# Block sums of the mixing weights by DRAM copies and adding transfers, four marking matmuls less, and a weighted product that waits

## The chip, the cores and the metric

The kernel runs on one core of a Trainium2 chip. The metric is the device time of one execution in microseconds (us), the median of several runs. TensorE (PE in the profile) does the matrix products, VectorE (DVE), ScalarE (ACT) and GpSimd (POOL) the rest; SyncE (SP) issues most transfers, ScalarE and GpSimd issue some. The engines run side by side, each its own instructions in a fixed order.

## The reference

Two branches read the normalised rows of x (2048 tokens of 512 values): a dilated local attention, and a gated MLP whose gate mixes tokens with the 2048 x 2048 weights `w_sp`.

```python
xn = _layernorm(x, axis=-1)
s = _A_ref(xn, A_wqkv, A_wo)            # 32 heads, 8 taps at a distance of 2, softmax, output product
g = _silu(_B_ref(xn, B_w_in, B_w_sp, B_b_sp, B_w_out))
return x + s * g

def _B_ref(x, w_in, w_sp, b_sp, w_out):
    z = _gelu(jnp.einsum("bsd,df->bsf", x, w_in))
    z1 = z[..., :Fh]
    z2 = _layernorm(z[..., Fh:], axis=-1)
    g = jnp.einsum("ts,bsf->btf", w_sp, z2) + b_sp[None, :, None]
    return jnp.einsum("bsf,fd->bsd", z1 * g, w_out)
```

## The kernel before

All products are made of three passes over values split in a high and a low half (`split`, L194: ScalarE makes the high half, VectorE subtracts it for the low one).

The opening (`opening`, L295, and the code around `column_tile`, L277) normalises x in 16 token tiles and turns them so that features lie on partitions. Tiles 0 to 5 are turned by TensorE. Tiles 6 to 15 come from a second, already turned copy of x (xT, L262); their means and scales are found on the rows (`row_stats`, L253), raised to a power on GpSimd (`rows_ready`, L267), stored to DRAM (`rows_out`, L240, tensor mv_d) and loaded back to all partitions (`rows_in`, L271, tile mr), in three sets: tiles 6 to 8, 9 to 12 and 13 to 15. `column_tile` then subtracts and multiplies (L280) and `low_x` (L234) makes the low half. `pair` (L427) makes the q, k and v products, group by group (g = 0, 1, 2, each with 512 columns of `wqkv`), and stores them to `qkv_d` from ScalarE's queue. TensorE takes the products in this order: group 0 for tiles 0 to 4, group 0 of tile 5 with group 1 of tiles 0 to 5, group 0 of tiles 6 to 15, group 1 of tiles 6 to 15, group 2 of all.

Then come the z1 products (L700 to L706), the z2 products (`z2_half`, L725, each half of a token tile's 896 columns in a bank: 512 and 384 wide), and the mixing with `w_sp`. The attention (`attention`, L530) runs on VectorE and GpSimd beside all of that, as a chain of operations in a fixed order (`line`); `weighted` (L618) multiplies the taps of v and notes each product in `sums_of`.

The mixing uses a scheme with seven products of blocks instead of eight: it needs, beside plain blocks of `w_sp`, four sums of blocks for each of two halves a of the output columns and each of eight token blocks. With t0, t1 for the upper and l0, l1 for the lower blocks, `added` (L390) makes

```python
for out_, p_, q_ in ((l1, t1, l1), (t1, t0, t1), (t0, t0, l1), (l0, t0, l0)):
    eng.tensor_tensor(out_, p_, q_, op=ALU.add)
```

`block_sums` (L395) loads the blocks, has them added and stores the results to `sums_d`. It is called three ways: `pool_sums` on GpSimd for six blocks of a = 1, behind column tile 12; `first_sums` on VectorE for a = 0, between the z1 products; `raw_sums` (L405) for the last two of a = 1, between the z2 products. The mixing loads the sums much later (`summed`, L872, from about 367 us on).

The mixing begins with `second_seeds` (L981): four matmuls without use of their results mark the banks of the second half (L984), and ScalarE then writes the biases into them as start values (`seed`, L843).

What sets the order: a scheduler places instructions by priority and by a simulated time line of its own, unless they are pinned (`pin`, `keep_in_program_order`) or held by a manual dependency. A transfer that nothing pins and that waits for nothing can be placed far ahead of where the code issues it. On each queue a transfer waits until the eighth before it has landed, and a queue's later transfers wait behind it.

Of the kernel before, what the change touches and what calls it, by code (L numbers as in the profile page):

```python
# [17 lines left out]
P = 128  # L18
# [39 lines left out]
def kernel(  # L58
# [330 lines left out]

    def added(ts, eng):  # L390
        t0, t1, l0, l1 = ts
        for out_, p_, q_ in ((l1, t1, l1), (t1, t0, t1), (t0, t0, l1), (l0, t0, l0)):
            eng.tensor_tensor(out_, p_, q_, op=ALU.add)  # L393

    def block_sums(a, i, tile_=None, eng=nc.vector, loads=nc.sync, stores=nc.scalar, behind=None):  # L395
        top, low = [(tile_ or t4)(f"s{n}_{a}_{i}") for n in "ab"]
        for t, r in ((top, 0), (low, HT)):
            ins = loads.dma_start(t, w_sp[2 * a : 2 * a + 2, r + i].rearrange("c p t -> p c t"))
            if behind:
                tc.add_manual_dep(ins.ins, behind[0].ins.name, behind[1], reason="sums later")  # L400
        added([top[:, 0], top[:, 1], low[:, 0], low[:, 1]], eng)
        for r, t in enumerate((top, low)):
            stores.dma_start(sums_d[a, r, i], t)

    def raw_sums(a, i):  # L405
        ts = [
            fetch(w_sp[2 * a + c, r + i], CT, f"sr_{a}_{i}_{c}_{r}") for r in (0, HT) for c in range(2)
        ]
        added(ts, nc.vector)
        for n, t in enumerate(ts):  # L410
            nc.sync.dma_start(sums_d[a, n // 2, i, :, n % 2], t)

    def early_tile(name):
        return t2(name).rearrange("p (i t) -> p i t", i=2)

    def pool_sums(a, i, tile_, *behind):
        block_sums(a, i, tile_, nc.gpsimd, nc.gpsimd, nc.gpsimd, behind)

    z1_sums = [(0, i) for i in range(HT)]

# [57 lines left out]
    for j in range(11, NT):  # L478
        if j + 2 < NT:
            fetch_cols(j + 2)  # L480
        if j == NT - 3:
            rb = raws.tile([P, 512], F32, tag="raw", name="rb", bufs=RAW)
            rbv = rb.rearrange("p (j q) -> p j q", j=JC)
            pin(nc.sync.dma_start(rbv, mv_d[:JC, 1].unsqueeze(0).to_broadcast([P, JC, P])))
        turned = column_tile(j)
        if j == 12:
            for i in range(HT - 2):
                pool_sums(1, i, early_tile, turned, SYNC)
        low_x(j - 1, cols[j - 1])
        if j % 2:  # L490
            pair(0, j - 5)
# [197 lines left out]

    def first_sums(a, i):  # L690
        block_sums(a, i, stores=nc.gpsimd)

    first_sums(*z1_sums[0])

    for f in range(FB):
        pair_ = side_pair("w1_last") if f == FB - 1 else None
        wh, wl = prep(w_in1[:, f, :], KB * P, f"w1_{f}", pair_=pair_)
        for c in range(NC):
# [11 lines left out]
            if c % 2:  # L710
                nc.scalar.dma_start(z1_d[f, c - 1 : c + 1].rearrange("c p t -> p c t"), zp)
        if f == 2:
            first_sums(*z1_sums[FB])
        if f < FB - 1:
            first_sums(*z1_sums[f + 1])

    HALF = (slice(0, 512), slice(512, FH))
    WID = (512, FH - 512)
    w2 = {
        (k, h): prep(w_in2[:, k, HALF[h]], WID[h], f"w2_{k}_{h}")  # L720
        for h in range(2)
# [3 lines left out]
    def z2_half(j, h, zt):  # L725
        xh, xl = xn_at(j)
        pz = mm(f"z2_{j}_{h}")[:, : WID[h]]
# [10 lines left out]
    def z2_stats(i, zts):  # L738
# [5 lines left out]
        mean, rstd = [mvz[:, i : i + HT + 1 : HT, n] for n in range(2)]  # L744
        nc.vector.tensor_scalar(rstd, rstd, EPS, None, op0=ALU.add)
        nc.gpsimd.tensor_tensor(rstd, rstd, nhalf.to_broadcast([P, 2]), op=ALU.pow)
# [33 lines left out]
    for i in range(HT + 2):  # L780
        if i in (1, 3):
            raw_sums(1, HT - 2 + i // 2)
        if i < HT:
# [76 lines left out]
    def plain(a, c, r):  # L860
        def w(s):
            js = r * HT + s
            pair_ = spatial.get((2 * a + c, js)) or spatial_block(2 * a + c, js)
            if (a, c, js) == (0, 0, 6):
                tc.add_manual_dep(
                    sums_of[9].ins, lows[-1].ins.name, NOSYNC, reason="first weights ahead"
                )
            return pair_

        return w  # L870

    def summed(a, half_, i):  # L872
        return lambda s: prep(sums_d[a, half_, s, :, i], CT, f"ws_{a}{half_}{i}_{s}")

# [106 lines left out]
    def second_seeds():  # L981
        for f in range(ODD + 1):

            nc.tensor.matmul(  # L984
                banks[1, f], z2_block(0, f)[0], half(0), start=True, stop=True
            )
        for f in range(ODD + 1):
# [191 lines left out]
```

## Time and profile before

| | us |
|---|---|
| median of 3 runs | 697.74 |
| lowest and highest | 696.59, 699.07 |
| profiled execution | 696.54 |
| its span, first to last instruction | 694.8 |
| granted TensorE clock | 1.00 |
| HBM read, written | 122.42 MB, 59.32 MB |
| DMA packets | 182.36 MB, mean 262 GB/s |

The page gives busy time by engine, the span in 40 slices of 17.4 us, the transfers by queue (q1 is SP's, q10 ScalarE's, q0 GpSimd's), the chain of work that ended last, and the costliest groups of instructions. A row of a group reads: line, engine, operation, output and input, count, busy us and mean ns of one, then the idle time of the engine before it and what ended it. A matmul of 512 columns is shown with 0.39 us, but they overlap: in the timeline one starts every 0.227 us.

### The profile page before, as it was taken

The page shows a single profiled execution, that of the slowest core. Times are in us where ns is not written, and L with a number is a line of the kernel's source. Part 1 is how long each engine was busy: PE and PEld are TensorE (multiplying, and loading weights), DVE is VectorE, ACT ScalarE, POOL GpSimd, SP SyncE. Part 2 cuts the span into 40 slices and gives each one's busy share as a digit, 9 for nine tenths or more (in the row PEclk, how much of TensorE's full clock was granted, in tenths as well). Part 3 has the DMA queues.
Part 4 walks back from the last instruction along what each step waited for, and adds up shares of the span by engine and source line. Part 5 has one row for each costly group of instructions (what it writes and reads, how often), then busy time and mean ns, then how long its engine had stood idle before and what let it go on. Part 6 is the DMA issues. An engine that isn't in the chain of part 4 may idle for free.

```text
span 694.8 us, 9233 instructions
## 1 busy us (share of the span) xinstructions
PE 686.6 (99%) x3084; PEld 573.0 (82%) x3084; DVE 619.4 (89%) x866; ACT 277.7 (40%) x458; POOL 215.2 (31%) x242
## 2 busy tenths in 40 slices
PE   8999999999999999998999999999999999999998
PEld 7888888888888899986888888888888888888886
DVE  6776868999989989889999998999989999989775
ACT  4342234224424256865534544442334444211531
POOL 3104837372343322124123222223111201642320
PEclk9999999999999999999999999999999999999999
DMA  8769899969999865267899768667576692655796
GB/s 270 252 193 289 288 348 384 346 204 358 407 412 340 329 231 190 80 201 231 258 403 314 284 211 298 208 232 248 183 261 206 215 342 89 221 173 190 246 330 235
DMA packets 102223, 182.36 MB, mean 262 GB/s; under 512 B 9184, under 2 KB 45280, under 8 KB 102176
## 3 DMA queue, kind: packets, MB, share of 16 engines
q1 hardware_dynamic: 56624, 102.21, 43.6%
q0 software_dynamic: 13824, 52.24, 20.9%
q10 hardware_dynamic: 31728, 27.33, 11.7%
q8 instruction: 24, 0.39, 0.2%
q14 instruction: 23, 0.19, 0.1%
HBM read 122.42 MB, written 59.32 MB: 262 GB/s over the span
## 4 chain that ended last, share of the span: by engine, by line
PE 67%; DVE 13%; DMA 12%; ACT 3%; issue 3%; POOL 1%; SPq 1%; DVEq 0%; POOLq 0%; ACTq 0%
PE g L825 35%; PE b L1067 4%; PE b L1069 4%; PE b L1068 4%; PE qkv L387 4%; PE qkv L386 4%; PE qkv L385 4%; DMA sb<-in_w_sp 3%; PE s L1069 2%; PE s L1068 2%; PE s L1067 2%; DMA sums_d<-sb 2%; DVE zst L742 2%; DMA z_d<-z1t 1%; DVE xT L280 1%
## 5 line engine op out<-in xcount | busy, mean ns | idle before, releaser
L633 POOL TENSOR_TENSOR pv<-pv 128x1024 f32<-128x1024 f32 x29 | 69.6, 2399 | 96.2 <-DVE pv L620 85.9
L573 DVE TENSOR_TENSOR pr<-k,q 128x2048 f32<-128x2048 f32 x32 | 73.6, 2299 | 2.0 <-DMA k<-qkv_d 1.9
L620 DVE TENSOR_TENSOR pv<-v,lg 128x2048 f32<-128x2048 f32 x32 | 74.6, 2331 | 0.7
L580 DVE TENSOR_REDUCE lg<-pr 128x128 f32<-128x2048 f32 x32 | 73.0, 2281 | 0.1
L647 POOL DMA_DIRECT2D o_d<-tt x32 | 18.0, 562 | 138.9 <-DVE tt L646 103.8
L433 ACT ACTIVATE stage<-qkv 128x512 f32<-128x512 f32 x40 | 23.0, 590 | 30.8 <-DMA qkv_d<-stage 17.0
L807 POOL DMA_DIRECT2D ol<-o_d x32 | 17.7, 555 | 37.7 <-DVE BIG L197 11.1
L1078 ACT ACTIVATE bt<-b 128x512 f32<-128x512 f32 x16 | 9.4, 599 | 43.5 <-PE b L1069 39.4
L709 ACT ACTIVATE z1t<-z 128x512 f32<-128x512 f32 x28 | 15.5, 597 | 26.1 <-DMA z_d<-z1t 15.3
L280 DVE TENSOR_TENSOR xT<-xT,mr 128x512 f32<-128x512 f32 x20 | 14.9, 743 | 11.9 <-DMA mr<-mv_d 6.4
L732 PE MATMUL z<-w_0h,BIG 128*128 128x512 f32 x64 | 25.0, 391 | 0.0
L731 PE MATMUL z<-w_0l,BIG 128*128 128x512 f32 x64 | 25.0, 391 | 0.0
L730 PE MATMUL z<-w_0h,BIG 128*128 128x512 f32 x64 | 24.9, 390 | 0.0
L742 DVE BATCH_NORM_STATS2 zst<-zt 128x6 f32<-128x448 f32 x32 | 19.3, 613 | 6.1 <-ACT zt L733 6.0
L754 ACT ACTIVATE zt<-zt,nmz,mvz 128x896 f32<-128x896 f32 x16 | 17.5, 1129 | 18.0 <-POOL nmz L748 18.0
L638 DVE TENSOR_TENSOR pv<-pv 128x512 f32<-128x512 f32 x32 | 22.9, 716 | 0.0
L733 ACT ACTIVATE zt<-z 128x512 f32<-128x512 f32 (+1 forms) x32 | 15.9, 536 | 15.2 <-DMA sums_d<-sa 14.0
L732 PE MATMUL z<-w_1h,BIG 128*128 128x384 f32 x64 | 21.5, 336 | 0.0
L730 PE MATMUL z<-w_1h,BIG 128*128 128x384 f32 x64 | 21.5, 335 | 0.0
L731 PE MATMUL z<-w_1l,BIG 128*128 128x384 f32 x64 | 21.4, 335 | 0.0
L393 POOL TENSOR_TENSOR sb<-sa,sb 128x512 f32<-128x512 f32 x12 | 19.7, 1644 | 5.4 <-DMA sb<-in_w_sp 5.1
L195 ACT ACTIVATE BIG<-zl 128x512 fp32r<-128x512 f32 x20 | 12.5, 630 | 21.6 <-DVE zl L895 19.8
(478 smaller groups left out, 2296.2 us busy)
## 6 DMA issues: line engine op xcount, KB each, us to landing
qkv_d<-stage ACTq DMA_DIRECT2D x24, 512.0 KB
v<-qkv_d POOLq DMA_DIRECT2D x14, 704.0 KB, 5.4
k<-qkv_d POOLq DMA_DIRECT2D x13, 704.0 KB, 6.8
sums_d<-sa POOLq DMA_DIRECT2D x14, 512.0 KB, 7.8
sums_d<-sb POOLq DMA_DIRECT2D x14, 512.0 KB, 8.0
z_d<-z1t ACTq DMA_DIRECT2D x14, 512.0 KB
zl<-z_d SPq DMA_DIRECT2D x12, 512.0 KB
tr<-t_d SPq DMA_DIRECT2D x12, 384.0 KB
```

The lines of the kernel that those rows point to most:

```text
L573: line(nc.vector.tensor_tensor(pr, taps(ks[u], j0), qb.unsqueeze(1).to_broadcast([P, W, NJ * CS]), op=ALU.mult))
L580: line(nc.vector.tensor_reduce(lgs[u][:, j0 * HS : (j0 + NJ) * HS].rearrange("p i w -> p w i"), pr.rearrange("p w (i d) -> p w i d", d=DH) ...
L620: line(nc.vector.tensor_tensor(pv.rearrange("p w (i d) -> p w i d", d=DH), taps(vs[u], j0).rearrange("p w (i d) -> p w i d", d=DH), lgs[u] ...
L633: eng.tensor_tensor(pv[:, 0:4], pv[:, 0:4], pv[:, 4:8], op=ALU.add)
L730: nc.tensor.matmul(pz, xh[:, k], wh, start=k == 0, stop=False)
L731: nc.tensor.matmul(pz, xh[:, k], wl, start=False, stop=False)
L732: nc.tensor.matmul(pz, xl[:, k], wh, start=False, stop=k == KB - 1)
L742: nc.vector.bn_stats(st[:, h], zt[:, h * FQ : (h + 1) * FQ])
L825: nc.tensor.matmul(pg, z[a], w[b], start=start and i == 0, stop=stop and i == 2, skip_group_check=seeded)
L1067: nc.tensor.matmul(pp[:, cols], hi, wh, start=k == 0, stop=False)
L1068: nc.tensor.matmul(pp[:, cols], hi, wl, start=False, stop=False)
L1069: nc.tensor.matmul(pp[:, cols], lo, wh, start=False, stop=k == n - 1)
```

## The change

1. `added`, `block_sums`, `raw_sums`, `pool_sums` and `first_sums` go, with their calls. The sums get 32 DRAM tensors of 512 KB, for a, the sum n, and pairs q of token blocks. A generator lists 64 transfers: `copied` copies a block pair from `w_sp` to a sum's tensor (DRAM to DRAM, on SP), `plus` adds a block pair, or another sum, to it (an adding transfer, on GpSimd). `go_on(n)` issues the next n of them.
2. `go_on` is called behind product pairs of groups 1 and 2 (13 times), behind the z1 products (28 times) and in the z2 loop (10 times with 2). These are 61; the last three of the list, which would add sum 0 to sum 2 for a = 1 and the pairs 1 to 3, are not issued, so these three tensors hold the lower block alone.
3. The marking matmuls go. In their place the first matmul of the narrow z2 halves of tiles 6, 7, 14 and 15 covers the whole bank: the weights of k = 0 are the last 512 columns instead of the last 384, and the half lies at the bank's end.
4. A manual dependency on VectorE puts the sixteenth weighted product of the attention behind the statistics of the last pair of z2 tiles. The old one, of the tenth, goes.

```diff
-    sums_d = dram.tile([2, 2, HT, P, 2, CT], F32, name="sums_d")
+    sums_d = {
+        (a, n, q): dram.tile([2, P, CT], F32, name=f"sums_{a}_{n}_{q}")
+        for a in range(2)
+        for n in range(4)
+        for q in range(HT // 2)
+    }
...
+    def rows_of_2k(blocks_):
+        return blocks_.rearrange("s p t -> (s p t)").rearrange("(r x) -> r x", x=4 * CT)
+
+    def raw_blocks(a, n, q):
+        r, c = divmod(n, 2)
+        j = r * HT + 2 * q
+        return w_sp[2 * a + c, j : j + 2]
+
+    def copied(to, a, q, src):
+        nc.sync.dma_start(rows_of_2k(sums_d[a, to, q]), rows_of_2k(src(a, q)))
+
+    def plus(to, a, q, src):
+        nc.gpsimd.dma_start(rows_of_2k(sums_d[a, to, q]), rows_of_2k(src(a, q)), accum_op=ALU.add, max_dma_last_dim=2048)
+
+    def weight_sums():
+        t0, t1, l0, l1 = [lambda a, q, n=n: raw_blocks(a, n, q) for n in range(4)]
+        s0, s3 = [lambda a, q, n=n: sums_d[a, n, q] for n in (0, 3)]
+        rounds = (
+            ((copied, 3, l1),),
+            ((copied, 0, t0), (plus, 3, t1)),
+            ((copied, 1, t0), (plus, 0, s3)),
+            ((copied, 2, l0), (plus, 1, t1)),
+            ((plus, 2, s0),),
+        )
+        for ops in rounds:
+            for a in range(2):
+                for q in range(HT // 2):
+                    for fn, to, src in ops:
+                        yield fn, to, a, q, src
...
+    def go_on(n):
+        for fn, *args in itertools.islice(coming_sums, n):
+            fn(*args)
...
-        turned = column_tile(j)
-        if j == 12:
-            for i in range(HT - 2):
-                pool_sums(1, i, early_tile, turned, SYNC)
+        column_tile(j)
...
             pair(g, j)
             pins[0] = False
+            go_on(1)
...
+        pz = bank[:, CT - WID[h] :]
         for k in range(KB):
-            wh, wl = [w[:, : WID[h]] for w in w2[k, h]]
-            nc.tensor.matmul(pz, xh[:, k], wh, start=k == 0, stop=False)
+            wh, wl = [w[:, CT - WID[h] :] if k == 0 else w[:, : WID[h]] for w in w2[k, h]]
+            if k == 0 and j % HT >= HT - 2:
+                nc.tensor.matmul(bank, xh[:, k], w2[k, h][0], start=True, stop=False)
+            else:
+                nc.tensor.matmul(pz, xh[:, k], wh, start=k == 0, stop=False)
...
-        nc.vector.tensor_scalar(rstd, rstd, EPS, None, op0=ALU.add)
+        known = nc.vector.tensor_scalar(rstd, rstd, EPS, None, op0=ALU.add)
+        if i == HT - 1:
+            tc.add_manual_dep(sums_of[15].ins, known.ins.name, NOSYNC, reason="gate rows ahead")
...
     def second_seeds():
-        for f in range(ODD + 1):
-
-            nc.tensor.matmul(
-                banks[1, f], z2_block(0, f)[0], half(0), start=True, stop=True
-            )
         for f in range(ODD + 1):
             seed(1, f, biases[1][0])
```

Where the scheduler puts the new transfers is not where the code calls `go_on`. On SP, at the start of the program (x are the row tiles, numbered by buffer; wqkv the weights of the second group; zpad zeros for a border), before:

```order
L202 DMA x_207<-in_x 128x512
L516 DMA qkv_d<-zpad 16x8x64 x2
L202 DMA x_209<-in_x 128x512
L202 DMA x_211<-in_x 128x512
L251 DMA x_213<-in_x 128x512
L251 DMA x_215<-in_x 128x512
L251 DMA x_217<-in_x 128x512
L251 DMA x_219<-in_x 128x512
L169 DMA wqkv_0r<-in_wqkv 128x512
```

and now, at the same place on SP (sums_3_0_93 is sum 3 of pair 0, with the buffer's number):

```order
L207 DMA x_238<-in_x 128x512
L404 DMA sums_3_0_93<-in_w_sp 16x8192
L404 DMA sums_3_1_94<-in_w_sp 16x8192
L404 DMA sums_3_2_95<-in_w_sp 16x8192
L207 DMA x_240<-in_x 128x512
L404 DMA sums_3_3_96<-in_w_sp 16x8192
L404 DMA sums_3_0_109<-in_w_sp 16x8192
L404 DMA sums_3_1_110<-in_w_sp 16x8192
L207 DMA x_242<-in_x 128x512
L256 DMA x_244<-in_x 128x512
L256 DMA x_246<-in_x 128x512
L256 DMA x_248<-in_x 128x512
```

Six copies now stand between the first row tiles and the weights of the second group, which follow four rows below this piece.

Further on SP, where the first set of row statistics is stored (mv_d) and loaded back (mr), before:

```order
L262 DMA xT_327<-in_x_t 128x512
L262 DMA xT_329<-in_x_t 128x512
L262 DMA xT_331<-in_x_t 128x512
L240 DMA mv_d<-mvt_335 6x32 x4
L271 DMA mr_361<-mv_d 128x768
L251 DMA x_363<-in_x 128x512
```

and now on SP, from the last of the copies ahead of that store on:

```order
L404 DMA sums_1_3_104<-in_w_sp 16x8192
L245 DMA mv_d<-mvt_366 6x32 x4
L404 DMA sums_2_0_89<-in_w_sp 16x8192
L404 DMA sums_2_1_90<-in_w_sp 16x8192
L404 DMA sums_2_2_91<-in_w_sp 16x8192
L404 DMA sums_2_3_92<-in_w_sp 16x8192
L404 DMA sums_2_0_105<-in_w_sp 16x8192
L404 DMA sums_2_1_106<-in_w_sp 16x8192
L404 DMA sums_2_2_107<-in_w_sp 16x8192
L404 DMA sums_2_3_108<-in_w_sp 16x8192
L276 DMA mr_392<-mv_d 128x768
```

All 32 copies now stand ahead of the first load of row statistics: 24 ahead of the store and eight between the two.

On GpSimd, the powers of the three sets (mvx, 128x3, 128x4 and 128x3) stood behind each other, with the sums' loads (sa, sb) after them:

```order
L214 TENSOR_TENSOR mvx<-mvx,nhalf 128x1 x5
L267 TENSOR_TENSOR mvx<-mvx,nhalf 128x3
L267 TENSOR_TENSOR mvx<-mvx,nhalf 128x4
L267 TENSOR_TENSOR mvx<-mvx,nhalf 128x3
L398 DMA sa_0_591<-in_w_sp 128x2x512
L398 DMA sb_0_592<-in_w_sp 128x2x512
```

and now on GpSimd the third power has the last adding transfers ahead of it:

```order
L407 DMA sums_2_0_89<-sums_0_0_81 256x512
L407 DMA sums_2_1_90<-sums_0_1_82 256x512
L407 DMA sums_2_2_91<-sums_0_2_83 256x512
L407 DMA sums_2_3_92<-sums_0_3_84 256x512
L407 DMA sums_2_0_105<-sums_0_0_97 256x512
L272 TENSOR_TENSOR mvx<-mvx,nhalf 128x3
L641 TENSOR_TENSOR pv_0_1252<-pv_0_1252 128x1024
```

Six of the 29 adding transfers stand ahead of the first power, six more ahead of the second, and the other seventeen ahead of the third; each waits on GpSimd for the copy into the same tensor, and for the sum that it reads, if it reads one.

More of the change, by code (lines that the diff above doesn't have):

```diff
@@ L388, in product @@
         return pq
[L390 to L403, printed above, removed]
@@ L719 @@
     w2 = {
[L720 removed]
+        (k, h): prep(
+            w_in2[:, k, slice(FH - CT, FH) if (k, h) == (0, 1) else HALF[h]],
+            CT if (k, h) == (0, 1) else WID[h],
+            f"w2_{k}_{h}",
+        )
         for h in range(2)
@@ L862, in w @@
             js = r * HT + s
[L863 to L866, printed above, removed]
-                )
-            return pair_
+            return spatial.get((2 * a + c, js)) or spatial_block(2 * a + c, js)
         return w
     def summed(a, half_, i):
-        return lambda s: prep(sums_d[a, half_, s, :, i], CT, f"ws_{a}{half_}{i}_{s}")
+        return lambda s: prep(sums_d[a, 2 * half_ + i, s // 2][s % 2], CT, f"ws_{a}{half_}{i}_{s}")
     def operand(i, s0):
```

27 lines of the change are left out of this document (4 added, 23 removed).

## The prediction

> **What bounds the kernel now.** I read the page first: the busy shares, the 40 slices, and the shares of the chain.
>
> ```profile
> PE 686.6 (99%) x3084; PEld 573.0 (82%) x3084; DVE 619.4 (89%) x866; ACT 277.7 (40%) x458; POOL 215.2 (31%) x242
> ...
> DMA  8769899969999865267899768667576692655796
> GB/s 270 252 193 289 288 348 384 346 204 358 407 412 340 329 231 190 80 201 231 258 403 314 284 211 298 208 232 248 183 261 206 215 342 89 221 173 190 246 330 235
> ...
> PE 67%; DVE 13%; DMA 12%; ACT 3%; issue 3%; POOL 1%; SPq 1%; DVEq 0%; POOLq 0%; ACTq 0%
> ```
>
> TensorE is busy nearly all the time, and two thirds of the chain are its own matmuls. The other third has to be looked for where TensorE waits. All its waits, from the view of who waited for whom:
>
> ```profile
> PE g L825 <- ACT g L843: 1.9, 1, 1.9
> PE warm L290 <- POOL ident masks.py:199: 1.3, 1, 1.3
> PE xt L228 <- DVE mvx L213: 0.7, 1, 0.7
> PE qkv L308 <- ACT BIG L229: 0.2, 1, 0.2
> PE g L825 <- ACT BIG L195: 0.2, 1, 0.2
> PE qkv L387 <- DVE BIG L234: 0.2, 1, 0.2
> ```
>
> After the first microseconds it waits 2.3 us in all. So a faster VectorE or emptier DMA queues can bring little, and anything that makes TensorE wait is paid in full, since its program order is fixed. Where it is nearest to waiting is the opening. The chain there, in order of time (start, us, what), is a relay of transfers and VectorE work that meets TensorE at 67.41 us:
>
> ```profile
> 24.81 0.88 POOL mvx L267
> ...
> 27.00 2.12 DMA mv_d<-mvt
> 29.13 4.68 DMA mr<-mv_d
> 33.90 0.70 DVE xT L280
> ...
> 36.74 0.60 DVE BIG L234
> ...
> 42.43 3.80 DMA mr<-mv_d
> ...
> 67.41 0.50 PE qkv L387
> ```
>
> Three times in the opening the row statistics go through a power on GpSimd (L267), a store to DRAM (mv_d) and a broadcast load (mr); only then can token tiles 6 to 8, then 9 to 12, then 13 to 15 be normalised (L280, L234) and multiplied. From the first power to a finished tile it takes 12.5 us (24.81 to 36.74 + 0.60, rounded). TensorE, in its timeline, takes up the product of tile 6 and that of tile 13 here:
>
> ```profile
> 43.24 0.39 PE L385 MATMUL qkv<-wqkv_0h,BIG 128*128 128x512 f32 x1
> ...
> 63.87 0.39 PE L385 MATMUL qkv<-wqkv_0h,BIG 128*128 128x512 f32 x1
> ```
>
> Tile 6 was ready at 37.3, so the slack there is 5.9 us; by tile 14 it is gone (the 0.2 us wait above).
>
> **The change part by part: the sums.** The 64 additions on VectorE and GpSimd go, with their loads and stores. Their rows:
>
> ```profile
> L393 DVE TENSOR_TENSOR sb<-sa,sb x16: 627/684/1003, 169.3 to 244.1; 128x512 f32<-128x512 f32 x16
> L393 POOL TENSOR_TENSOR sb<-sa,sb x12: 1279/1329/3334, 63.8 to 148.1; 128x512 f32<-128x512 f32 x12
> ```
>
> VectorE ran 40 of them, 40 x 0.684 = 27 us, GpSimd 24, about 37 us. None stood on TensorE's path between 70 and 310 us, where it never waits, so this relief is worth at most the 2.1 us of waits at L825.
>
> In their place come 32 copies DRAM to DRAM of 0.524 MB on SP and 29 additions of the same size issued by GpSimd. What decides is where they stand. They depend on nothing but each other, and the order shows all of them in the opening: six copies ahead of the second weight group, all 32 ahead of the first broadcast load (mr of tile 6), and all 29 additions ahead of the third power on GpSimd, which tiles 13 to 15 need. Both queues run in order. The engines were not free there; windows of the whole run, with busy us, then clock, DMA share and GB/s last:
>
> ```profile
> 0.00:60.00 60.00, 57.67 (x262) 47.31 (x263) 38.70 (x88) 23.22 (x38) 12.35 (x20) 1.00 0.77 238
> 60.00:250.00 190.00, 189.79 (x853) 158.82 (x852) 174.06 (x201) 60.77 (x107) 92.24 (x92) 1.00 0.94 338
> ```
>
> A share of 0.77 leaves 0.23 x 60 = 14 us of engine time. The new work is several times that. Prices, from the queues:
>
> ```profile
> q1 hardware_dynamic: 56624, 102.21, 43.6%
> q0 software_dynamic: 13824, 52.24, 20.9%
> q10 hardware_dynamic: 31728, 27.33, 11.7%
> ```
>
> A load on q1: 43.6% of 694.8 us is 303 us for 102.21 MB, 337 GB/s, so 256 KB (0.262 MB) take 0.78 us of all 16 engines. A 512 KB store on q10 takes 1.56 us in the same way. No row has DRAM on both sides. **Bounds of a copy:** not under 0.524 MB at the fastest slice of the page, 412 GB/s, which is 1.27 us; not over twice that, 2.55 us, if its read and its write both count against those 412. I take the middle, 1.9 us, since loads and stores, the two nearest rows, each resemble one half of it. **Bounds of an addition**, which reads two operands and writes one: from a plain transfer, 1.27 us, to two slow copies, 5.1 us; the middle is 3.2 us, for the same reason.
>
> The Trainium skill, "DMA: Bandwidth & Descriptors", section "Latency and other measured facts", gives 207 to 214 GB/s per direction for copies between HBM tensors; by that a copy takes 2.5 us, an estimate, and the sum below would be about 19 us longer. No run here shows it yet.
>
> **The sum.** Ahead of the third power stand 25 loads (19.5 us), six stores of the first products (9.4), 32 copies (32 x 1.91 = 61) and, with up to eight additions in flight when the last is issued (each waits for the eighth before it), about 25 additions (25 x 3.2 = 80). From a start at 2 us that is 172 us; 12.5 us later, at 184.5, a tile is ready. TensorE wanted tile 13 at 63.9: a shift of 121 us. The first broadcast load gives the same by another way: the additions follow the copies in turns, so about 21 of them (67 us) are served by the time the 32nd copy is: 2 + 28.9 + 61 + 67 = 159, then 4.7 us for the load and 3.5 to the tile, 167, against 43.2: 124 us. These do not add, since a late first table delays the third too but its time passes while the additions run. I take **122 us**. TensorE can do nothing meanwhile, because everything behind product 6 needs products in the fixed order; later weights and the attention move with it. The earlier delay, of the second weight group behind six copies and their additions, lies inside this wait.
>
> **The marking matmuls, the wide halves, the weighted product.** The timeline has the marking matmuls back to back:
>
> ```profile
> 311.49 1.07 PE L984 MATMUL g<-BIG 128*128 128x512 f32 x4
> 312.39 0.39 PE L825 MATMUL g<-wsp_6h,BIG 128*128 128x512 f32 x1
> ```
>
> Their going saves 312.39 - 311.49 = 0.9 us of TensorE. Four first matmuls grow from 384 to 512 columns; the groups say 335 against 390 ns, so 4 x 0.055 = 0.2 us. If the seeds then come sooner, and VectorE is freer, the 2.1 us of waits at L825 may go; I give all of it: 0.9 + 2.1 - 0.2 = 2.8 us gained. The wait put on the 16th weighted product is free, by these VectorE starts:
>
> ```profile
> 304.04 2.29 DVE L620 TENSOR_TENSOR pv<-v,lg 128x2048 f32<-128x2048 f32 x1
> ...
> 318.58 0.16 DVE L745 TENSOR_SCALAR mvz<-mvz 128x2 f32<-128x2 f32 x1
> ```
>
> When the last gate statistics were done, at 318.58, only the tenth product had run, so the sixteenth comes later anyhow, unless the 27 us freed bring the attention six steps forward. Then the attention behind it on VectorE (its folds, GpSimd's and the output stores) pauses, but VectorE has 694.8 - 619.4 = 75 us of idle time to make it good.
>
> Sum: profiled execution 696.5 (span 694.8 and 1.7 around it; the median of the runs, 697.7, is 0.2% above) + 122 - 2.8 = **816 us**.
>
> **The rivals.** First, two reads at memory-bound copies: an addition costs two copies and a copy 2.55 us. Then the third power comes at 2 + 28.9 + 81.6 + 127.5 = 240, the tile at 252.5, the shift is 189, the time 882 us. For it: an addition has an operand more to read than any transfer of this trace, and the slices stop at 412 GB/s. Against: slices at that rate also stand at a DMA digit of 9, so the engines, not the memory, may be the limit. The Trainium skill, "Collectives: The Full Stack", section "The bandwidth ceiling: the fold count and why AG ≠ RS ≠ AR", says that an add in the DMA path is slow by its two source reads, not by the adding, and halves the rate; no run here shows it, and it leans to this rival.
>
> Second, the copies yield nothing to the additions: if engines serve SP's ring first and both prices are the lowest, the first tile is ready at 2 + 28.9 + 40.6 + 4.7 + 3.5 = 79.7, a shift of 36 us; the third gate, with 25 x 1.27, still gives 2 + 28.9 + 40.6 + 31.8 + 12.5 - 63.9 = 52 us, so 746 us. That is the low end.
>
> Third, on the other side: the early transfers are hidden. The place is the first table; the slack is 5.9 us and the free engine time 14 us, so it decides if 32 copies and the additions beside them pass in 20 us, 0.3 us for each of 61. The kernel then takes 696.5 - 2.8 = 694 us. For it: TensorE has its relief at L825 whatever the sums do. Against: 61 x 0.524 MB in 20 us are 1600 GB/s, four times the page's best slice. The same time would come out if the change did what its text says and put one transfer behind each product pair; the order says it doesn't.
>
> **How the numbers follow.** The forecast's own case, prices between the bounds: 0.78. Two reads at memory-bound copies, 882 us: 0.13. A part hidden, between 700 and 745 us: 0.05. Hidden: 0.04, of which 0.01 for a gain too small to tell, since a measurement of this kernel tells about 0.3%. The range runs from the low end, 745, to 885, just over the rival, because a 512 KB addition has no row of its own. Chances: faster 0.03, within 0.3% 0.01, slower 0.96.
>
> **What would show it.** Right: the waits of TensorE show over 100 us in the opening, the longest before products of tiles 6 to 15; the first mr lands after 100 us; the slices of DMA are full from the start for some 150 us; from there on the timeline is that of before, shifted, without L984 and without the wait of 1.9 us. Wrong: mr lands before 60 us (prices below the bounds, or rings that let small transfers past), or the shift is made at GpSimd alone, with the first table on time. A time over 885 us would mean additions beyond two slow copies each.

## The result, and the profile after

The changed kernel takes **894.9 us** (median of 4 runs, 893.98 to 897.82) where the kernel before takes 697.69 (median of 4): 1.283 times as long, interval 1.279 to 1.287. The profiled run took 893.98 us, its span is 892.2. One of the four executions of e8 below, the profiled one, took 1794 us, with its matmuls over twice as long as otherwise; it is left out, and no row of e8 is shown.

On the page of the changed kernel stand the busy shares, then from the 40 slices (22.3 us each now) TensorE, the granted clock (PEclk, in tenths) and the DMA engines, and the shares of the chain:

```profile
PE 700.3 (78%) x3080; PEld 580.5 (65%) x3080; DVE 575.1 (64%) x826; ACT 288.3 (32%) x464; POOL 191.0 (21%) x207
...
PE   6105603000599999999997899999999999999998
...
PEclk9556956555699999999999899999999999999999
DMA  9994977565567767664052569886866586635394
...
PE 58%; issue 18%; DMA 11%; DVE 7%; POOL 4%; ACT 2%; SPq 0%; DVEq 0%; POOLq 0%; ACTq 0%
```

TensorE has four matmuls fewer, as planned. Its row has become a stretch of eleven slices with holes, then the old picture with one dent (7, 8). In those eleven slices the DMA engines are full in four only (the first three and the fifth) and have room in the others, while TensorE still waits: the transfers' engine time alone cannot explain the hole. In the chain "issue", time in which an engine waits for nothing that the profile shows, has grown from 3% to 18%.

All waits of TensorE over 2 us, from the view of who waited for whom (us, times, longest):

```profile
PE qkv L392 <- DVE BIG L239: 106.6, 2, 91.3
PE xt L233 <- DVE mvx L218: 47.4, 2, 46.4
PE qkv L390 <- ACT BIG L288: 14.1, 1, 14.1
PE qkv L313 <- ACT BIG L234: 9.5, 2, 9.2
PE g L834 <- ACT g L852: 6.3, 2, 3.7
PE g L834 <- ACT wsp_5h L200: 2.8, 1, 2.8
```

Five waits of 9 us and more in the opening (91.3, 46.4, 15.3, 14.1, 9.2), and 9.1 us at the mixing's line, where the 2.1 us of before were expected to go. Two of VectorE's own waits, in the same view, say what stands behind the largest:

```profile
DVE mvt L243 <- POOL mvx L272: 113.5, 3, 92.2
DVE x L195 <- POOL mvx L219: 48.9, 1, 48.9
```

VectorE waits for powers on GpSimd: 92.2 us for the one of the third set (L272), 48.9 us for the small one of row tile 4 (L219). GpSimd's timeline shows what the powers wait behind (start, us, operation, idle time before it):

```profile
223.92 0.90 POOL L407 DMA_DIRECT2D sums<-sums  x1 [4.89 <-issue]
229.62 0.89 POOL L407 DMA_DIRECT2D sums<-sums  x1 [4.80 <-issue]
230.20 1.22 POOL L272 TENSOR_TENSOR mvx<-mvx,nhalf 128x3 f32<-128x3 f32 x1
```

One adding transfer each 5.7 us: 0.9 to issue it, 4.8 in which GpSimd does nothing and nothing behind it starts. From 110.97 us on 21 additions come so, 21 x 5.7 = 119 us up to the third power; the eight before them took longer, beside the copies. The list of transfers says how long one is under way (KB, median us from issue to landing), and how much of the engines GpSimd's queue took:

```profile
q0 software_dynamic: 15952, 46.47, 21.7%
...
sums<-in_w_sp POOLq DMA_DIRECT2D x16, 512.0 KB, 5.8
...
sums<-sums POOLq DMA_DIRECT2D x13, 512.0 KB, 5.4
```

A landing takes as long as the period, and the trace's DMA packets show why. An addition's first packet starts 1.6 us after its issue, its 256 packets of 2 KB take some 3.4 us, and in 23 of the 28 gaps the next issue comes 0.64 to 0.69 us after the last of them has ended. So GpSimd issues an addition when the one before has landed.

The delay is split by two marks, the first z2 product and the first output product, in the view of a tile's groups (first and last start behind the durations). Before:

```profile
L731 PE MATMUL z<-w_0l,BIG x64: 389/389/397, 218.0 to 290.5; 128*128 128x512 f32 x64
...
L1067 PE MATMUL b<-wout_0h,BIG x16: 389/389/389, 570.8 to 642.2; 128*128 128x512 f32 x16
```

and in the changed kernel:

```profile
L739 PE MATMUL z<-w_0l,BIG x64: 389/389/397, 403.8 to 476.3; 128*128 128x512 f32 x64
...
L1066 PE MATMUL b<-wout_0h,BIG x16: 389/389/389, 768.2 to 839.6; 128*128 128x512 f32 x16
```

**The opening** is 403.8 - 218.0 = 185.8 us late. **The stretch** from the first z2 product to the first output product, called so from here on, takes 364.4 us instead of 352.8, 11.6 more. Together 197.4, all of the loss.

### The profile page after: what moved, and what is told of

It reads as the page before. It is cut to its first block, busy times and chain, and to the rows that moved or that the text cites. A ratio compares the mean times of both kernels' runs of the same rounds, so it can differ in the third digit from the quotient of the medians.

```text
span 892.2 us, 9097 instructions
## 1 busy us (share of the span) xinstructions
PE 700.3 (78%) x3080; PEld 580.5 (65%) x3080; DVE 575.1 (64%) x826; ACT 288.3 (32%) x464; POOL 191.0 (21%) x207
## 3 DMA queue, kind: packets, MB, share of 16 engines
q0 software_dynamic: 15952, 46.47, 21.7%
## 4 chain that ended last, share of the span: by engine, by line
PE 58%; issue 18%; DMA 11%; DVE 7%; POOL 4%; ACT 2%; SPq 0%; DVEq 0%; POOLq 0%; ACTq 0%
PE g L834 21%; PE qkv L392 4%; PE qkv L390 3%; PE qkv L391 3%; PE z L707 3%; PE z L706 3%; PE b L1066 3%; PE b L1067 3%; PE b L1068 3%; PE z L708 3%; POOL sums L407 2%; DMA x<-in_x 2%; DMA qkv_d<-stage 2%; PE s L1067 2%; PE s L1068 2%
## 5 line engine op out<-in xcount | busy, mean ns | idle before, releaser
L392 PE MATMUL qkv<-wqkv_0h,BIG 128*128 128x512 f32 x43 | 17.7, 411 | 106.6 <-DVE BIG L239 106.6
L392 PEld LDWEIGHTS qkv<-wqkv_0h,BIG 128*128 128x128 f32 x43 | 8.3, 192 | 109.7 <-DVE BIG L239 108.1
L243 DVE STREAM_TRANSPOSE mvt<-mvx 128x32 f32<-128x32 f32 x3 | 0.6, 211 | 113.5 <-POOL mvx L272 113.5
L288 ACT ACTIVATE BIG<-xT 128x512 fp32r<-128x512 f32 x10 | 6.3, 633 | 121.1 <-DVE xT L285 120.6
L233 PE MATMUL xt<-ident,x 128*128 128x128 f32 x24 | 4.2, 305 | 47.6 <-DVE mvx L218 47.4
L407 POOL DMA_DIRECT2D sums<-in_w_sp x16 | 14.7, 922 | 102.7 <-issue 92.6
L233 PEld LDWEIGHTS xt<-ident,x 128*128 128x128 f32 x24 | 3.1, 157 | 49.6 <-DVE x L195 47.1
L195 DVE TENSOR_SCALAR x<-x,mvx 128x512 f32<-128x512 f32 x2 | 1.1, 546 | 48.9 <-POOL mvx L219 48.9
L407 POOL DMA_DIRECT2D sums<-sums x13 | 11.7, 900 | 76.6 <-issue 55.4
L390 PE MATMUL qkv<-wqkv_0h,BIG 128*128 128x512 f32 x43 | 16.6, 401 | 14.1 <-ACT BIG L288 14.1
L740 PE MATMUL z<-w_0h,BIG 128*128 128x512 f32 x64 | 25.0, 391 | 0.0
```

Source lines behind the costliest of these rows:

```text
L390: nc.tensor.matmul(pq, xh[:, k], wh, start=k == 0, stop=False)
L392: nc.tensor.matmul(pq, xl[:, k], wh, start=False, stop=k == KB - 1)
L407: nc.gpsimd.dma_start(rows_of_2k(sums_d[a, to, q]), rows_of_2k(src(a, q)), accum_op=ALU.add, max_dma_last_dim=2048)
```

## The experiments

The opening's lateness and the stretch are read from the same two rows in every run. The kernel before ran beside each group: 694.86 us beside e1 to e4, 695.14 beside e5 to e8, 694.79 beside e9 to e12.

| run | median us | ratio to before (interval) | opening late | stretch |
|---|---|---|---|---|
| changed kernel | 894.9 | 1.283 (1.279 to 1.287) | 185.8 | 364.4 |
| e3 copies alone | 764.2 | 1.100 (1.096 to 1.104) | 48.6 | 369.7 |
| e1 additions in 8 KB pieces | 830.0 | 1.194 (1.192 to 1.197) | 122.7 | 363.6 |
| e11 additions in 4 KB pieces | 829.0 | one run | 121.9 | 363.4 |
| e2 additions behind the powers | 847.8 | 1.220 (1.216 to 1.224) | 136.9 | 364.3 |
| e4 one for each product | 771.6 | 1.109 (1.105 to 1.113) | -0.5 | 428.5 |
| e8 e4 with 8 KB pieces | 719.4 | 1.035 (1.032 to 1.037) | - | - |
| e10 e8 with the old wait | 709.0 | 1.021 (1.018 to 1.023) | -0.3 | 368.3 |
| e5 before, marks alone | 694.3 | 0.999 (0.9975 to 1.0005) | -0.8 | 350.8 |
| e6 before, marks and wait | 709.6 | 1.021 (1.019 to 1.022) | -0.8 | 366.9 |
| e7 changed, no wait | 890.2 | 1.280 (1.277 to 1.283) | 185.3 | 362.9 |
| e9 changed, old wait | 877.5 | 1.263 (1.260 to 1.265) | 183.7 | 349.3 |
| e12 changed, room for the power | 879.9 | 1.268 (1.263 to 1.274) | 183.0 | 353.2 |

### What the copies cost: e3

```diff
     def plus(to, a, q, src):
-        nc.gpsimd.dma_start(rows_of_2k(sums_d[a, to, q]), rows_of_2k(src(a, q)), accum_op=ALU.add, max_dma_last_dim=2048)
+        pass
```

> The changed kernel without the 29 additions: the sums hold the copied block alone. It shows the cost of the 32 copies on SP's queue by itself. Theory A: an opening 35 to 45 us late as in the run with the additions behind the powers, 720 to 745 us in all. If the prediction's price of a copy held, 1.9 us, it would be 55 to 60 us late and take 750 to 755 us. For the mixing: if the 10 us lost there come from the waiting weighted product, the missing marking matmuls or VectorE's new timing, they are lost here too (z1 to end shifted by 10 us more than the opening); if they come from the additions they are gone.

Measured: 764.2 us, the opening 48.6 us late. SyncE's timeline has the issue of the first load of row statistics, and the page the share of GpSimd's queue without additions:

```profile
73.14 0.36 SPq L276 DMA_DIRECT2D mr<-mv_d  x1
...
q0 software_dynamic: 8064, 31.27, 12.5%
```

When this load was issued, the last copies were still under way, so its time alone does not give their price. The trace's DMA packets do: the copies' are the only ones of 32 KB, 512 of them, the last of which ends at 79.7 us. Together they took 46.2 us of all 16 engines, 1.44 us a copy, 0.524 MB / 1.44 us = 364 GB/s; in the changed kernel they took 44.3 us, 1.38 us a copy, 380 GB/s. That is near theory A's price and nearer to the prediction's lowest bound (1.27) than to its 1.9. The lateness lies between the two expectations (35 to 45, and 55 to 60), and the time is above both, because the stretch is 17 us longer than before. There is no adding transfer in this program, so the adding transfers do not make the changed kernel's loss in the mixing.

### Why GpSimd waits: e1 and e11

The additions in larger, fewer pieces; the data and the bytes are the same.

```diff
-accum_op=ALU.add, max_dma_last_dim=2048)
+accum_op=ALU.add, max_dma_last_dim=8192)
```

> The changed kernel with additions in pieces of 8 KB instead of 2 KB (64 instead of 256 pieces each); nothing else differs. Theory A, that the pieces of one addition fill the room that GpSimd has for its transfers' descriptors, so that the next issue waits until the one before has drained: with a quarter of the pieces several additions fit, the 4.8 us of idle time behind each issue go while fewer than about four are in flight, the third power comes when the engines have done the work, at 120 to 160 us instead of 230, and the kernel takes 790 to 825 us. Theory B, that GpSimd waits for each adding transfer to land whatever its pieces: idle time of 3 us or more stays behind every issue, the period falls only by what larger pieces save (5.7 to 4 us at the least), the third power comes at 180 us or later, and the kernel takes 845 to 895 us.

> The changed kernel with additions in 128 pieces of 4 KB, between the 256 pieces of 2 KB and the 64 of 8 KB. Theory A (GpSimd has room for a fixed number of pieces, one addition of 256 of them): two additions fit, so issues come two at a time, an addition lands about two periods after its issue (with 2 KB pieces one period, 5.7 us), the period is 2.8 to 4 us, and the kernel takes 830 to 860 us. Rival C (each piece costs GpSimd or the engines a fixed time, one addition after the other, 5.7 us / 256 = 22 ns): the period is 2.9 us as well, but an addition has landed before the next is issued, within 3 to 4 us of its own issue.

Measured: 830.0 us with 8 KB, 5 us above theory A's range and 15 below theory B's, and 829.0 with 4 KB, 1 us below theory A's. With 8 KB the third power came at 162.08 us, again just behind what theory A expected. Two neighbours in GpSimd's timeline of the 8 KB kernel, its queue's share, the landing times, and the row of ScalarE's timeline that ends its longest wait:

```profile
105.50 0.79 POOL L407 DMA_DIRECT2D sums<-sums  x1 [1.87 <-issue]
108.01 0.78 POOL L407 DMA_DIRECT2D sums<-sums  x1 [1.72 <-issue]
...
q0 software_dynamic: 10384, 46.47, 20.9%
...
sums<-in_w_sp POOLq DMA_DIRECT2D x16, 512.0 KB, 18.0
...
sums<-sums POOLq DMA_DIRECT2D x13, 512.0 KB, 25.9
...
154.74 1.26 ACT L443 ACTIVATE stage<-qkv,mvx 128x512 f32<-128x512 f32 x2 [71.69 <-DMA qkv_d<-stage]
```

The same of the 4 KB kernel:

```profile
147.99 0.82 POOL L407 DMA_DIRECT2D sums<-sums  x1 [1.93 <-issue]
150.78 0.81 POOL L407 DMA_DIRECT2D sums<-sums  x1 [1.97 <-issue]
...
sums<-sums POOLq DMA_DIRECT2D x13, 512.0 KB, 8.0
```

The period falls from 5.7 to 2.8 and 2.5 us, while one addition is under way for 8.0 and for 18 to 26 us: about three in flight with 4 KB (8.0 / 2.8), seven or more with 8 KB (18.0 / 2.5), one with 2 KB. The fewer the pieces, the more of them overlap. Theory B and rival C, one addition after the other, are out. Theory A, room for a fixed number of pieces, fits in its direction, but not in number: it expected two in flight with 4 KB. No run gave GpSimd a larger room, so that a room for pieces is what holds it is inferred from the piece counts and not shown.

Where the additions overlap, the sum of the engines' time fits. The share of GpSimd's queue less that of the run without additions gives an addition's price: (20.9% x 828.3 - 12.5% x 760.3) / 29 = 2.7 us in 8 KB pieces, and (21.7% x 892.2 - 12.5% x 760.3) / 29 = 3.4 us in 2 KB pieces. Then 2 + 28.9 + 32 x 1.38 + 29 x 2.7 = 153 us of transfers, and at 154.74 a store of 512 KB has landed for which ScalarE, and TensorE behind it, had waited 71.7 us.

### Where the transfers stand: e2, e4, e8, e10

In e2 only the additions move, behind the third power on GpSimd:

```diff
-        nc.gpsimd.dma_start(...)
+        ins = nc.gpsimd.dma_start(...)
+        tc.add_manual_dep(ins.ins, powers[-1].ins.name, NOSYNC, reason="additions behind the powers")
```

> The changed kernel with all 29 additions put behind the third power on GpSimd; the 32 copies stay where they are. Theory A (GpSimd, held by one addition after the other, made most of the shift): only the copies are left in front, the first load of row statistics waits for 25 loads and stores of 28.9 us and 32 copies of 1.25 to 1.4 us, 40 to 45 us, so it lands near 75 to 80 instead of 33.8 us, the opening is 35 to 45 us late, and the kernel takes 725 to 750 us, some 10 us of it lost later, in the mixing. Rival (the engines' time made the shift, wherever it is spent, as the prediction had it): the additions, now issued from about 75 us on, load the engines just as long, 29 x 2.9 = 84 us, the tables of tiles 9 to 15 come late once more, and the kernel takes over 780 us.

Measured: 847.8 us. The rival's number, but neither theory's reason. The waits of VectorE and of GpSimd:

```profile
DVE pv L648 <- POOL pv L643: 93.3, 1, 93.3
...
POOL sums L408 <- issue: 147.8, 26, 9.9
```

The powers now come in time (the third at 91.03), and GpSimd then stands 147.8 us between its additions all the same. The attention's first fold (L643) is queued behind all 29 and starts at 279.62; VectorE waits 93.3 us for it, and TensorE waits 79.6 us in one piece in the z1 products, for ScalarE, where an exponential of the attention (idle time before it 86.4 us) stands ahead of their results. As in the changed kernel, the held queue costs what stands next behind it: there a power, here a fold.

In e4 every transfer waits for the newest product where the code calls for it, as the change's text reads:

```diff
+        tc.add_manual_dep(ins.ins, newest[-1].ins.name, SYNC, reason="one for each product")
```

> The changed kernel with each transfer held behind the newest product's eviction where the code calls for it, so that none stands in the opening: the first follow the third weight group's products, the last the z2 products. Theory A (the place makes the whole shift): no wait of TensorE over 1 us before 67 us, the opening as before the change, and 690 to 710 us in all, with up to 10 us lost in the mixing if these do not come from the early transfers. Rival: the additions cost as much anywhere, since each holds GpSimd some 5 us, 29 x 5.7 = 165 us, and the attention's folds and the gate's powers queue behind them: 720 us or more, with the waits of TensorE in the z2 products and the mixing.

Measured: 771.6 us, the rival. The opening is as before (-0.5 us), so the place does make the opening's delay. But TensorE now waits further on:

```profile
PE z L743 <- DVE w_1l L203: 27.2, 2, 23.4
PE g L838 <- ACT BIG L201: 17.2, 1, 17.2
PE z L742 <- ACT zt L745: 10.4, 1, 10.4
```

e8 is e4 with pieces of 8 KB:

> The changed kernel with both cures at once: each transfer behind the newest product, and additions in pieces of 8 KB. Theory A (two faults, the place of the transfers and the small room for descriptors): no issue holds GpSimd for over 2 us except where it waits for a product or a copy, the waits of TensorE in the z2 products (37.6 us in the run with 2 KB pieces) fall under 10 us, and the kernel takes 700 to 725 us. Rival (the transfers' waits on GpSimd for a product and for a copy hold the attention, whatever the pieces): 755 us or more.

Measured: 719.4 us, the median of three runs (716.83 to 721.27), inside theory A's range. So 52 us of e4's loss go with the 2 KB pieces; which waits went is not shown, since e8 has no row here.

e10 is e8 with the old wait of the tenth weighted product (below):

> All three cures: each transfer behind the newest product, additions in pieces of 8 KB, the old wait of the tenth weighted product. If place, pieces and the missing wait are the whole of the 197 us, 697 to 710 us are left, 10 to 15 us under the run without the old wait (720.3 us); what stays above the kernel before is GpSimd waiting for products and copies with the attention's folds queued behind. Rival (something else in the transfers' way costs as well): 715 us or more.

Measured: 709.0 us, as expected, 10 us under e8 and 14 us over the kernel before. The opening is as before, and the stretch is 15.5 us longer: at the mixing's start ScalarE waits for the first weights, which are loaded beside the last additions (ScalarE's timeline):

```profile
323.07 0.64 ACT L201 ACTIVATE wsp_2h<-wsp_2r 128x512 fp32r<-128x512 f32 x1 [6.31 <-DMA wsp_2r<-in_w_sp]
328.15 0.63 ACT L201 ACTIVATE wsp_3h<-wsp_3r 128x512 fp32r<-128x512 f32 x1 [4.45 <-DMA wsp_3r<-in_w_sp]
334.54 0.63 ACT L201 ACTIVATE wsp_4h<-wsp_4r 128x512 fp32r<-128x512 f32 x1 [5.34 <-DMA wsp_4r<-in_w_sp]
```

That the additions make these loads late is argued from the times; no run took them apart.

### The 11.6 us in the mixing: e5, e6, e7, e9, e12

e5 is the kernel before with the third part of the change (marking matmuls gone, wide halves), e6 has the fourth part as well:

> The kernel before with the third part of the change alone: the marking matmuls go, four narrow z2 halves begin 512 wide. The prediction gave this 0.9 - 0.2 = 0.7 us, and up to 2.1 us more where the seeds come sooner: 692 to 694.5 us where the kernel before takes 694.9. Rival for the 11.6 us that the changed kernel lost in the mixing (M1, the missing marking matmuls reorder the mixing's start): 700 us or more, with waits of TensorE of 5 us or more at the mixing's line.

> The kernel before with the third and the fourth part of the change, without the block sums by transfers: the sixteenth weighted product waits for the last gate statistics, too. The prediction had this wait free: as the run with the third part alone, within 1 us. Rival M2 (the wait takes time from the attention or from the weights' split at the mixing's start): 3 us or more above that run. If both runs stand near 694 us, the loss of 11.6 us in the mixing comes from the first part, through VectorE's new timing without its 40 additions (M3).

Measured: 694.3 us for e5, 0.8 less than before beside it, which its interval does not tell from nothing; the stretch is 2.0 us shorter. 709.6 us for e6. The fourth part, called free in the prediction, costs 15.3 us on the kernel before. The rows of e6:

```profile
L739 PE MATMUL z<-w_0l,BIG x64: 389/389/628, 217.2 to 294.2; 128*128 128x512 f32 x64
...
L1067 PE MATMUL b<-wout_0h,BIG x16: 389/389/389, 584.1 to 655.5; 128*128 128x512 f32 x16
```

The fourth part is two edits: a wait on the sixteenth weighted product comes, the old one on the tenth goes. e7 takes the new one out of the changed kernel, e9 puts the old one back instead:

```diff
-        if i == HT - 1:
-            tc.add_manual_dep(sums_of[15].ins, known.ins.name, NOSYNC, reason="gate rows ahead")
...
+            if (a, c, js) == (0, 0, 6):
+                tc.add_manual_dep(
+                    sums_of[9].ins, lows[-1].ins.name, NOSYNC, reason="first weights ahead"
+                )
```

> The changed kernel without the wait of the sixteenth weighted product (and without the old one of the tenth). The opening stays as in the changed kernel, 185.8 us late at the first z2 product. If the wait makes the loss in the mixing (M2), the kernel takes 883 to 887 us; if VectorE's timing without its additions makes it (M3), the gate's power on GpSimd is still held for several us and the time stays at 892 to 900 us.

> The changed kernel with its fourth part undone: the tenth weighted product waits for the first mixing weights again, and the sixteenth for nothing. Theory M4 (the loss in the mixing comes from the old wait that went: without it the attention runs on through the z2 products and keeps VectorE full, and GpSimd's gate powers and the last gate rows come late): the attention pauses at the tenth product, no gate power takes over 2 us, from the first z2 product to the first output product pass 351 to 355 us as before the change instead of 364.6, and the kernel takes 881 to 887 us. Rival M3 (VectorE's timing without its additions, or the shifted state): 362 us or more for that stretch, and 892 us or more in all.

Measured: 890.2 us for e7, between the two expectations, its stretch only 1.5 us shorter. 877.5 us for e9, better than M4 expected:

```profile
L739 PE MATMUL z<-w_0l,BIG x64: 389/389/397, 401.7 to 474.2; 128*128 128x512 f32 x64
...
L1069 PE MATMUL b<-wout_0h,BIG x16: 389/389/390, 751.0 to 822.4; 128*128 128x512 f32 x16
```

Its stretch is 349.3 us, 15.1 less than in the changed kernel and 3.5 less than before, and TensorE's 9.1 us of waits at the mixing's line are gone. So it is the old wait's going that costs. With the old wait VectorE makes no weighted product between these two, while the z2 products run:

```profile
373.44 2.29 DVE L628 TENSOR_TENSOR pv<-v,lg 128x2048 f32<-128x2048 f32 x1
481.83 2.29 DVE L628 TENSOR_TENSOR pv<-v,lg 128x2048 f32<-128x2048 f32 x1
```

In the changed kernel it makes six of them there, the first and the last being

```profile
386.96 2.29 DVE L628 TENSOR_TENSOR pv<-v,lg 128x2048 f32<-128x2048 f32 x1
462.44 2.27 DVE L628 TENSOR_TENSOR pv<-v,lg 128x2048 f32<-128x2048 f32 x1
```

beside the z2 products' statistics and the gate rows. M3 is out: e6 still has VectorE's additions and loses the time, e9 lacks them and does not. The longest gate power on GpSimd goes the same way: 1.68 us before, 1.69 in e5 and 1.68 in e9, as M4 expected, but 7.43 in the changed kernel and in e7, and 6.24 in e6.

What of that delays TensorE was asked by e12, which leaves the order of waits and ties VectorE's combinations of gate blocks to the newest power on GpSimd:

```diff
             nc.vector.tensor_tensor(out_, p_, q_, op=op)
...
+            tc.add_manual_dep(ins.ins, powers[-1].ins.name, SYNC, reason="room for the power")
```

> The changed kernel with the combinations of gate blocks on VectorE behind the newest gate power on GpSimd, so that VectorE pauses while GpSimd has such a power to do. Theory L (GpSimd cannot begin while VectorE reads two operands from SBUF without a pause; in the changed kernel one power of 256 values took 7.43 us, until VectorE's next gap): no gate power takes over 2.7 us, ScalarE's wait for it (5.8 us) goes, and the mixing wins back 3 to 8 us: 887 to 892 us. Rival (the power is slow for another reason, or off the path): one power still takes 5 us or more, or the time stays within 2 us of 894.9.

Measured: 879.9 us, so more was won back than expected, while one power still took 5.29 us. In the changed kernel, GpSimd's longest power and two rows of VectorE's timeline, the last ahead of its next gap and the first behind it:

```profile
475.57 7.43 POOL L756 TENSOR_TENSOR mvz<-mvz,nhalf 128x2 f32<-128x2 f32 x1 [8.36 <-DVE mvz L753]
...
481.76 0.67 DVE L202 TENSOR_TENSOR wsp_4l<-wsp_4r,wsp_4h 128x512 fp32r<-128x512 f32 x1
486.12 0.69 DVE L202 TENSOR_TENSOR BIG<-zt,BIG 128x512 fp32r<-128x512 f32 x1 [3.68 <-ACT BIG L200]
```

and in e12 the last row ahead of VectorE's pause, and the one that waits for the power (GpSimd's power ran from 471.65 for 5.29 us):

```profile
475.69 0.67 DVE L203 TENSOR_TENSOR wsp_2l<-wsp_2r,wsp_2h 128x512 fp32r<-128x512 f32 x1
476.97 0.56 DVE L778 TENSOR_TENSOR zt<-zt 128x384 f32<-128x384 f32 x1 [0.60 <-POOL mvz L757]
```

Both powers end 0.57 us or so after VectorE falls idle (481.76 + 0.67, 483.00; 475.69 + 0.67, 476.94), as if they got nowhere while VectorE ran one operation of two operands after another. The Trainium skill, "SBUF — State Buffer", section "SBUF: two separate sides", has a rule for that: one pair of ports serves GpSimd and such VectorE operations, as an exclusive lock for a whole instruction. These rows agree. But e9's power at 474.03 took 1.08 us in a stretch of VectorE just as full, so what decides when GpSimd gets in is open, and so is why e12 wins 11 us back although its longest power shrank by 2 us only. In the changed kernel the chain of work goes over the long power, by ScalarE's and VectorE's work on the gate rows, to the matmul at 490.53 us for which TensorE had waited 2.53 us. What is shown is that the stretch takes 362.9 us or more in every profiled run without the old wait, and 349.3 to 352.8 with it (before, e5, e9), or 353.2 with the gate blocks tied to the powers (e12). The one run with the old wait and a long stretch is e10, 368.3 us; there no power takes over 1.08 us, and additions stand beside the mixing's first weights.

## Why the prediction failed, by its own steps

**What bounds the kernel: right.** TensorE's order is fixed, the opening is nearest to waiting, and what is late there is paid: the opening's waits are 106.6 + 47.4 + 14.1 + 9.5 = 177.6 of 185.8 us. The rest is mostly slow matmuls behind these waits, which the prediction left out (last section): up to the first z2 product TensorE is busy 224.7 us instead of 215.5.

**The step that failed** is the additions' term: "with up to eight additions in flight when the last is issued (each waits for the eighth before it), about 25 additions (25 x 3.2 = 80)". Not eight were in flight but one. The price of one on the engines was right, 3.4 us where 3.2 were taken, but GpSimd was held 5.7 us for each, so the third power came at 230.2 us instead of 172, and everything else queued on GpSimd was held as well. That includes a wait that the prediction did not see: the small power of row tile 4, behind six additions, for which TensorE stood 46.4 us. With pieces of 4 and 8 KB, where additions do overlap, the opening is 121.9 and 122.7 us late, against a forecast of 122. That agreement is partly luck, as the next two steps show. One addition at a time is worth 185.8 - 122.7 = 63 us.

**The copies' price was too high**: 1.38 us where 1.91 were taken, in the bounds (1.27 to 2.55). 32 x 0.53 = 17 us too many. The Trainium skill's 207 to 214 GB/s, "DMA: Bandwidth & Descriptors", section "Latency and other measured facts", would have made it 2.5; it is for rows of 16 KB that lie 512 KB or more apart, and here, with rows that follow each other, the trace shows 380 GB/s. Alone, the copies make the opening 48.6 us late.

**The path from the third power to TensorE was another.** It was to be 12.5 us, over store and load to tile 13. TensorE's last wait ended at 233.62, 3.4 us behind the power, and for tile 8: on VectorE the transposition of the third set (L243) stands ahead of the next column tiles in program order and waits for the power. In the 8 KB run not a table but a store of products, behind which ScalarE stood, came last. The sum of transfers was the same.

**Marks and wide halves: not contradicted**, 0.7 us forecast, 0.8 measured in e5, below what a measurement tells. **The relief at L825 came only with the old wait in place**: 2.8 us forecast in all, 3.5 us shorter in e9's stretch.

**The weighted product's wait was priced on the wrong half.** "Free" was worked out for the wait that comes. The one that goes was named in the change and given no price, and it costs 15.3 us on the kernel before (e6 against e5) and 15.1 us of the changed kernel's stretch (364.4 - 349.3), of which the new wait makes at most 1.5 (e7). The row on which "free" rested, only ten products run when the last statistics were done, was itself made by the old wait. The prediction had even written down the condition, that the attention comes forward, but looked for its cause in the 27 us that VectorE saves. It looked at who waits for the attention and not at what the attention, let loose, takes VectorE from.

So the 78.9 us between 816 and 894.9 are 185.8 - 122 = 63.8 in the opening and 11.6 + 2.8 = 14.4 in the stretch, with 0.7 left. **The rivals**: the first, at 882 us, came near in time with a mechanism that did not act: it priced a copy at 2.55 us and an addition at 5.1. An addition did cost about two copies, and more in 2 KB pieces, on the engines (2.7 and 3.4 us against 1.38), which agrees with the two source reads of the Trainium skill's "Collectives: The Full Stack", section "The bandwidth ceiling: the fold count and why AG ≠ RS ≠ AR". The second was near in the copies' price alone; the third, hidden transfers, is out. Of the signs to watch, "the shift is made at GpSimd alone, with the first table on time" was half right: the shift was made at GpSimd, with the first table late too (VectorE has it at 110.86 us). Two of the signs for "right" came although the step was wrong, waits of over 100 us in the opening and a first table after 100 us; the third, full engines for some 150 us, did not. Nor did a time over 885 us mean additions beyond 5.1 us each: they took 3.4 on the engines, and the rest was GpSimd standing still.

## What to carry to other kernels

A transfer that an engine issues has two prices, its time on the DMA engines and the time for which the issuing queue is held; where the second isn't shown by a row, ask what stands behind it on that queue, and try few large pieces against many small ones, as the 4 and 8 KB runs did here. A dependency that is taken away needs a price as much as one that is added: find what it kept back and which engine that will now fill. A transfer that waits for nothing should be held where it is wanted, and then its last neighbours looked at: e10's 14 us seem to be lost to weights loaded beside the last additions.

## What the hardware showed that was not expected

- Adding transfers of 512 KB in 256 pieces of 2 KB went one at a time, 5.7 us each, and held GpSimd 4.8 us of it, also where they were nearly alone on the DMA engines (e2, 206 to 279 us: 4.7 us, at a DMA share of 0.57). In 4 or 8 KB pieces three, and seven or more, were in flight.
- A DRAM-to-DRAM copy of 512 KB in contiguous rows took 1.38 to 1.44 us of all 16 DMA engines, 364 to 380 GB/s.
- After the wait of 91.32 us TensorE was slow for some 3.5 us (its timeline):

```profile
234.64 0.63 PE L391 MATMUL qkv<-wqkv_1l,BIG 128*128 128x512 f32 x1
235.07 0.63 PE L392 MATMUL qkv<-wqkv_1h,BIG 128*128 128x512 f32 x1
...
237.40 0.39 PE L392 MATMUL qkv<-wqkv_3h,BIG 128*128 128x512 f32 x1
237.63 0.39 PE L390 MATMUL qkv<-wqkv_0h,BIG 128*128 128x512 f32 x1
```

  One starts every 0.43 us there, at a granted clock of 0.51 (233.6 to 237.2 us), and every 0.23 us from 237.4 on, at 1.00. This wait costs some 1.6 us (8 matmuls at 0.2 us more) beyond its own length. The mixing's waits that ended at 490.53 and 510.03 us, 2.53 and 3.73 us long, were followed by such stretches too, of 14 and 8 matmuls.
- A gate power of 256 values on GpSimd took 7.43 us beside a full VectorE in the changed kernel, 1.08 us beside one just as full in e9, and 0.7 us at the least.
